# Two sparse-attention and MLP layers on one core: four rounds of the first MLP cut into three ranges of inner blocks, and the weight conversion spread to match

## The chip, the cores and the metric

One core of one Trainium2 chip runs the whole program. The metric is the device time of one execution in microseconds (us); lower is better. Where the text says PE, DVE, ACT, POOL and SP, it means the tensor, vector, scalar, GpSimd and sync engines, as the profile does.

## The reference

```python
# attention: q, k, v are [4, 8, 576, 64]
scores = scale * q @ k.T
thresh = max(scores, axis=-1) - tau
scores = where(scores >= thresh, scores, -1e9) - max(scores)
attn = exp(scores) / (sum(exp(scores)) + 1e-9)
x = (attn @ v)  ->  [2304, 512]
# first MLP, 512 -> 2048 -> 512
h = x @ w_in
g = where(h >= 1, h, where(h <= -1, 0, (h + 1)**2 / 4))
x = g @ w_out
# second MLP, other weights
h = x @ w_in2
g = h * clip(h + 3, 0, 6) / 6
out = g @ w_out2
```

## The kernel before

**Attention.** There are 16 jobs, one for a batch and a pair of heads, and each has five blocks of query rows. One block of one job is here called a step: 80 steps, 0 to 79, with job j at steps 5j to 5j+4. In a step PE makes the scores (L335), DVE copies them out with a minimum of the negated scores (L348), ACT takes the exponential (L360), DVE masks and sums (L369), PE transposes the result through the identity (L284), ACT copies that out (L397 and others) and PE multiplies with v (L433). A job has nine tiles of scores, so nine L348 and nine L369; the profile records a second short read of the accumulator for each.

**First MLP beside attention.** While attention still runs, the program works on six groups of 256 rows (groups 0 and 1 are batch 0, 2 and 3 batch 1, 4 and 5 batch 2). A round is one group with a list of inner blocks, each 128 of the 2048 hidden columns; only blocks 0 to 9 are treated in this part. For each inner block, `em_h` makes the hidden tile on PE in 12 matmuls of 256 columns (L676; three products for each of four slices, since values are split into a high and a low part), and ACT, DVE and POOL make its activation (L685 to L694). Two `em_part` calls then multiply it with the output weights, 6 matmuls each (L738), one for each half of the output columns. These add up over the round in one PSUM bank, "Q3". At the end of a half the sum is copied out and stored to `x2p` (L747 to L752). If the round's first block isn't block 0, the earlier partial sum is loaded first into the one buffer `before` (L732) and added at the copy (L747). At the start of a round `split_x` makes the high and low part of the group's rows: four pairs of ACT L656 and DVE L657, into buffers that the round before has to have left. The sequence of blocks over all rounds is numbered n = 0 to 59.

**How the two are woven.** The attention code is a generator; at each of its yields (22 in five steps) the MLP generator `dense1` gets a credit of 0.57, and each slice of its work costs 0.33, so that a block n with two output parts costs 2.64. Before a round of a group, `dense1` asks `ready(g)`: all four jobs of the group's batch must have been normalized. Batch 1 is jobs 4 to 7, and the last of them is normalized at step 44. Until then `dense1` yields nothing, and the credit is cut at 3. What is left when attention ends runs after it without attention beside it. A scheduler then moves instructions within each engine's order.

**Weights.** Each inner block needs a piece of the input weights and one of the output weights, 20 pieces in this part. They arrive as 64-bit floats and are converted on the chip: ACT L118, L121, L139, POOL L122, L137, L141, DVE L129 and L135. `pace(n)` says how many pieces are to be done at block n: `FIRST` before the first block, then `RATE` for each block.

**After attention.** The rest of the groups and the second MLP follow with matmuls of 512 columns (L676, L718) from about 500 us to the end.

Of the kernel before, what the change touches and what calls it, by code (L numbers as in the profile page):

```python
# [18 lines left out]
def kernel(  # L19
# [24 lines left out]
    NG = (NB - 1) * MAIN // GRP  # L44
# [3 lines left out]
    NF1 = 10  # L48
# [22 lines left out]
    def narrow(t, g):  # L71
        return t[g // 2][:, :, (g % 2) * GRP:(g % 2 + 1) * GRP]
# [594 lines left out]
    def em_h(key, m, f):  # L667
        cnt["h"] += 1
        n = GRP if key[2] == 1 else WIDE[key[1]]
        h = bank(H_TAGS[cnt["h"] % len(H_TAGS)])[:, 0:n]  # L670
        wh, wl = wsp["i", m, f]
        x = 0
        for kk in range(KD):
            xh, xl = xs[key][kk]
            for l, r in ((wh, xh), (wh, xl), (wl, xh)):
                mm = T.matmul(h, l[:, kk * 128:(kk + 1) * 128], r, start=(x == 0), stop=(x == 3 * KD - 1))  # L676
                if x % 3 == 0:
                    pin_mlp(mm)
                x += 1
            if kk < KD - 1:  # L680
                yield 0.33
        hp_, hb = (mt, HOLD) if key[2] == 1 else (wide["g"], MLAG + 1)
        r = hp_.tile([128, n], F32, tag="r", name="r", bufs=2)
        if m == 0:
            S.activation(out=r, in_=h, func=ACTF.Relu, scale=0.5, bias=half)  # L685
            S.activation(out=r, in_=r, func=ACTF.Square)  # L686
            vlast = V.scalar_tensor_tensor(out=r, in0=r, scalar=1.0, in1=h, op0=ALU.min, op1=ALU.max)  # L687
        else:
            S.activation(out=r, in_=h, func=ACTF.Relu, bias=three)  # L689
            vlast = V.scalar_tensor_tensor(out=r, in0=r, scalar=6.0, in1=h, op0=ALU.min, op1=ALU.mult)  # L690
        gh = hp_.tile([128, n], F32R, tag="gh", name="gh", bufs=hb)
        gl = hp_.tile([128, n], F32R, tag="gl", name="gl", bufs=hb)
        x = S.activation(out=gh, in_=r, func=ACTF.Copy)  # L693
        y = G.tensor_tensor(out=gl, in0=r, in1=f32(gh), op=ALU.subtract)  # L694
        gs[key, f] = (gh, gl)
        if not mode["att"]:
            pins.update(S=x, V=vlast, G=y)
# [24 lines left out]
    def em_part(key, half, f):  # L722

        gh, gl = gs[key, f] if half == 0 else gs.pop((key, f))
        wh, wl = wsp["o", 0, f]
        g, fs = ROUNDS[key[3]]
        dst = narrow(x2p, g)[:, 2 * half:2 * half + 2, :]
# [61 lines left out]
                nc.sync.dma_start(out=out[b * SEQ + MAIN:(b + 1) * SEQ, :], in_=ob[64 * e:64 * e + 64, :])  # L789

    HALF = NF1 // 2
    ROUNDS = [(g, list(range(f, f + HALF))) for f in (0, HALF) for g in range(2)]
    ROUNDS += [(g, list(range(NF1))) for g in range(2, NG)]
    before = {}
    hs = [(r, f) for r, (g, fs) in enumerate(ROUNDS) for f in fs]
    n_h = len(hs)
    outs = [(r, half, f) for r, (g, fs) in enumerate(ROUNDS) for half in range(2) for f in fs]
    OFF = NF1 + 2 * MLAG - 3
    steps, o = [], 0
    while o < len(outs):  # L800
        n = len(steps)
# [8 lines left out]
    def round_key(r):  # L810
        return (0, ROUNDS[r][0], 1, r)

    def dense1(ready, ahead):

        for n, l in enumerate(steps[:n_h]):
            r, f = hs[n]
            key = round_key(r)
            if key not in xs:
                while not ready(key[1]):
                    yield None  # L820
                split_x(key)
            ahead(n, f)
            yield from em_h(key, 0, f)
            if f == ROUNDS[r][1][-1]:
                xs.pop(key)
                if r + 1 < len(ROUNDS) and ready(ROUNDS[r + 1][0]):
                    split_x(round_key(r + 1))
            if n == n_h - 3 and not mode["att"]:
                split_x((0, NB - 1, 2))
            yield 0.33  # L830
            for i, (r, half, f) in enumerate(l):
                if i == 1:
                    pace(n + 0.5)
                yield from em_part(round_key(r), half, f)
                yield 0.33
# [86 lines left out]
    by_use = sorted(first_use, key=lambda x: (first_use[x], x))  # L922
    weights.items += [(kind, 0, f) for kind, f in by_use]

    def pace(n):
        goal = min(2 * len(by_use), 2 * FIRST + 2 * RATE * n)
        while mode["att"] and 2 * weights.done + weights.mid < goal:
            weights.half()

    def ahead1(n, f):  # L930
        weights.upto(sum(1 for x in by_use if first_use[x] < n + 2))
        pace(n)
        if not mode["att"] and weights.done < 2 * KF:
            weights.half()

    part1 = dense1(ready, ahead1)
    share = 0.57
    FIRST, RATE = 5, 0.85
    credit = 0.0
    for _ in attention():  # L940
        if not mode["mlp"]:
# [110 lines left out]
```

## Time and profile before

| what | value |
|---|---|
| median of 3 runs | 1119.37 us (1119.02 to 1120.56) |
| the profiled execution's own time | 1118.67 us |
| its span, first to last instruction | 1116.9 us |
| PE busy | 1087.4 us (97%) |
| DVE, ACT, POOL busy | 583.3, 614.0, 438.4 us |
| granted TensorE clock, mean | 0.992 |

Matmuls are pipelined, so that a busy PE isn't the same as a PE that starts a matmul as often as it can; how far apart the matmuls start is read from the chain of work in order of time. The stretches used below begin at the first DVE row L348 of steps 24, 39, 44 and 78: at 102.5, 207.3, 237.8 and 445.4 us.

### The profile page before, as it was taken

The page shows a single profiled execution, that of the slowest core. Times are in us where ns is not written, and L with a number is a line of the kernel's source. Part 1 is how long each engine was busy: PE and PEld are TensorE (multiplying, and loading weights), DVE is VectorE, ACT ScalarE, POOL GpSimd, SP SyncE. Part 2 cuts the span into 40 slices and gives each one's busy share as a digit, 9 for nine tenths or more (in the row PEclk, how much of TensorE's full clock was granted, in tenths as well). Part 3 has the DMA queues.
Part 4 walks back from the last instruction along what each step waited for, and adds up shares of the span by engine and source line. Part 5 has one row for each costly group of instructions (what it writes and reads, how often), then busy time and mean ns, then how long its engine had stood idle before and what let it go on. Part 6 is the DMA issues. An engine that isn't in the chain of part 4 may idle for free.

```text
span 1116.9 us, 17595 instructions
## 1 busy us (share of the span) xinstructions
PE 1087.4 (97%) x6478; PEld 882.1 (79%) x6478; DVE 583.3 (52%) x1204; ACT 614.0 (55%) x1215; POOL 438.4 (39%) x382
## 2 busy tenths in 40 slices
PE   7998889999999999999999999999999999999998
PEld 5555667777878877888889888888888888898886
DVE  5899887876666656355536765558411111211111
ACT  5777886866667666556557766555432222333222
POOL 0233767622222111155627566567522222222221
PEclk9999889999999999999999999999999999999999
DMA  6454445433222110025222544533010110010001
GB/s 165 118 100 107 124 120 150 103 93 74 63 59 62 43 43 22 12 67 170 77 94 78 157 143 145 158 114 111 24 38 1 33 38 1 10 38 8 13 1 38
DMA packets 140230, 84.26 MB, mean 75 GB/s; under 512 B 99440, under 2 KB 123248, under 8 KB 140144
## 3 DMA queue, kind: packets, MB, share of 16 engines
q1 hardware_dynamic: 138800, 82.84, 27.0%
q8 instruction: 51, 0.84, 0.3%
q10 hardware_dynamic: 1344, 0.30, 0.1%
q14 instruction: 35, 0.29, 0.1%
HBM read 65.73 MB, written 17.37 MB: 74 GB/s over the span
## 4 chain that ended last, share of the span: by engine, by line
PE 88%; DVE 7%; ACT 2%; POOL 1%; issue 1%; SPq 1%; DMA 0%; DVEq 0%; POOLq 0%; ACTq 0%
PE Q L676 35%; PE P L718 28%; PE Q L738 7%; PE Q L433 6%; PE P L335 6%; PE Q L284 5%; DVE p L348 2%; DVE p L369 2%; ACT e L360 1%; DVE xl L657 1%; SPq L227 0%; PE Q L904 0%; DVE th L363 0%; DVE w_c L135 0%; DMA w_raw<-in_moe_w_out_dram 0%
## 5 line engine op out<-in xcount | busy, mean ns | idle before, releaser
L694 POOL TENSOR_TENSOR gl<-r,gh 128x512 fp32r<-128x512 f32 (+1 forms) x190 | 202.6, 1067 | 501.0 <-ACT gh L693 500.5
L676 PE MATMUL Q<-xh,wih 128*128 128x512 f32 (+1 forms) x760 | 262.0, 345 | 0.9 <-DVE r L687 0.7
L676 PE MATMUL Q<-xl,wih 128*128 128x512 f32 (+1 forms) x760 | 257.1, 338 | 0.0
L676 PE MATMUL Q<-xh,wil 128*128 128x512 f32 (+1 forms) x760 | 256.8, 338 | 0.0
L690 DVE SCALAR_TENSOR_TENSOR r<-r,Q 128x512 f32<-128x512 f32 (+1 forms) x80 | 50.7, 633 | 249.4 <-ACT r L689 249.3
L693 ACT ACTIVATE gh<-r 128x512 fp32r<-128x512 f32 (+1 forms) x190 | 99.9, 526 | 125.3 <-PE P L718 53.2
L676 PEld LDWEIGHTS Q<-xh,wih 128*128 128x128 f32 x760 | 144.1, 190 | 24.3 <-issue 4.2
L676 PEld LDWEIGHTS Q<-xl,wih 128*128 128x128 f32 x760 | 144.2, 190 | 16.0
L676 PEld LDWEIGHTS Q<-xh,wil 128*128 128x128 f32 x760 | 144.0, 190 | 15.5
L348 DVE TENSOR_SCALAR_CACHE_REDUCE p<-P 128x576 f32<-128x576 f32 x144 | 104.0, 751 | 53.3 <-PE Q L284 41.0
L369 DVE SCALAR_TENSOR_TENSOR p<-p,th,e 128x576 f32<-128x576 f32 x144 | 122.8, 873 | 15.1 <-ACT e L360 9.5
L689 ACT ACTIVATE r<-Q,three 128x512 f32<-128x512 f32 (+1 forms) x80 | 51.4, 643 | 142.9 <-PE Q L676 138.3
L360 ACT ACTIVATE e<-p,nm 128x576 f32<-128x576 f32 x144 | 108.9, 775 | 34.5 <-DVE p L348 33.6
L687 DVE SCALAR_TENSOR_TENSOR r<-r,Q 128x256 f32<-128x256 f32 (+1 forms) x110 | 54.8, 498 | 125.7 <-ACT r L686 122.4
L284 PE MATMUL Q<-ident,p 128*128 128x128 f32 x656 | 107.9, 282 | 9.8 <-ACT Gf L397 6.5
L718 PE MATMUL P<-woh,gh 128*128 128x512 f32 x288 | 111.9, 390 | 0.6 <-DVE ob L776 0.6
L718 PE MATMUL P<-wol,gh 128*128 128x512 f32 x288 | 112.2, 390 | 0.0
L718 PE MATMUL P<-woh,gl 128*128 128x512 f32 x288 | 111.0, 390 | 0.0
L335 PE MATMUL P<-kt,qt 64*128 64x288 f32 (+1 forms) x640 | 99.5, 429 | 11.0 <-DVE p L348 9.0
L284 PEld LDWEIGHTS Q<-ident,p 128*128 128x128 f32 x656 | 73.6, 141 | 46.3 <-ACT Gf L397 14.0
L137 POOL TENSOR_TENSOR w_c<-w_c,w_raw 128x512 int32<-128x512 int32 x64 | 89.5, 1400 | 41.3 <-DVE w_c L135 23.0
L397 ACT ACTIVATE Gf<-Q 128x512 f32<-128x512 f32 x128 | 74.4, 596 | 33.5 <-PE Q L284 32.8
(91 smaller groups left out, 1840.1 us busy)
## 6 DMA issues: line engine op xcount, KB each, us to landing
w_raw<-in_moe_w_in_dram SPq DMA_DIRECT2D x32, 512.0 KB
w_raw<-in_moe_w_out_dram SPq DMA_DIRECT2D x32, 512.0 KB
vn<-in_v_dram SPq DMA_DIRECT2D x32, 128.0 KB
x2p<-ob SPq DMA_DIRECT2D x16, 256.0 KB
x2d<-ob SPq DMA_DIRECT2D x16, 256.0 KB
xst<-x2d SPq DMA_DIRECT2D x16, 256.0 KB
out_dram<-ob SPq DMA_DIRECT2D x16, 256.0 KB
xst<-xd SPq DMA_DIRECT2D x15, 256.0 KB
```

What stands on the lines that cost most here:

```text
L137: x = G.tensor_tensor(out=c.bitcast(I32), in0=c.bitcast(I32), in1=r, op=ALU.add)
L284: x = T.transpose(out, in_, ident)
L335: mm = T.matmul(o, qt[j][r, c], kt[j][r, k0:k0 + HS], start=True, stop=True, skip_group_check=True)
L348: reads(V.tensor_scalar(out=p[:, x], in0=s[:, :, 0:HS], scalar1=-1.0, scalar2=3e38, op0=ALU.mult, op1=ALU.min, accum_out=nm[:, x:x + 1]), ...
L360: pins["S"] = S.activation(out=e, in_=p[:, x], func=ACTF.Exp, bias=nm[:, x:x + 1], scale=-1.0)
L369: pins["M"] = V.scalar_tensor_tensor(out=p[:, x], in0=p[:, x], scalar=th[:, x:x + 1], in1=e, op0=ALU.is_le, op1=ALU.mult, accum_out=zt[j][ ...
L397: S.activation(out=f[:, h, :, d0:d0 + 128], in_=tm.rearrange("p (c n) -> p c n", c=4), func=ACTF.Copy)
L676: mm = T.matmul(h, l[:, kk * 128:(kk + 1) * 128], r, start=(x == 0), stop=(x == 3 * KD - 1))
L693: x = S.activation(out=gh, in_=r, func=ACTF.Copy)
L694: y = G.tensor_tensor(out=gl, in0=r, in1=f32(gh), op=ALU.subtract)
L718: T.matmul(a, l, r, start=(first and x == 0), stop=(last and x == 2))
L738: mm = T.matmul(o, l, r, start=(f == fs[0] and x == 0 and i == 0), stop=(f == fs[-1] and x == 2 and i == 1), skip_group_check=True)
```

## The change

Rounds 0 to 3 were (group 0, blocks 0 to 4), (1, 0 to 4), (0, 5 to 9), (1, 5 to 9), and groups 2 to 5 had all ten blocks in one round each. Now the rounds are (0, 0 to 3), (1, 0 to 3), (0, 4 to 6), (1, 4 to 6), (2, 0 to 6), (3, 0 to 6), then 7 to 9 for groups 0, 1, 2 and 3, then groups 4 and 5 as before: 12 rounds in place of 8, with the same 60 blocks n. The conversion's pace is 0.75 for a block up to n = 12 and 0.45 behind it, in place of 0.85.

```diff
     HALF = NF1 // 2
-    ROUNDS = [(g, list(range(f, f + HALF))) for f in (0, HALF) for g in range(2)]
-    ROUNDS += [(g, list(range(NF1))) for g in range(2, NG)]
+    PLAN = (((0,1),0,4),((0,1),4,7),((2,3),0,7),((0,1,2,3),7,10))
+    ROUNDS = [(g, list(range(a, z))) for gs_, a, z in PLAN for g in gs_]
+    ROUNDS += [(g, list(range(NF1))) for g in range(4, NG)]
...
     def pace(n):
-        goal = min(2 * len(by_use), 2 * FIRST + 2 * RATE * n)
+        goal = min(2 * len(by_use), 2 * FIRST + 2 * RATE * min(n, KNEE) + 2 * LATER * max(n - KNEE, 0))
...
-    FIRST, RATE = 5, 0.85
+    FIRST, RATE, KNEE, LATER = 5, 0.75, 12, 0.45
```

The first block of group 2 was n = 20 and is now n = 14. On PE, before, step 41 begins with the scores (L335), v (L433), a transpose (L284), and then has the 12 matmuls of a hidden tile (L676):

```order
L335 MATMUL P_2946<-kt,qt 128x288
L335 MATMUL P_2947<-kt,qt 128x288
L335 MATMUL P_2946<-kt,qt 128x288
L335 MATMUL P_2947<-kt,qt 128x288
L433 MATMUL Q_2896<-Gf,vn_97 64x320 x8
L433 MATMUL Q_2896<-Gt,vn_97 64x320 x2
L284 MATMUL Q_2914<-ident,p 128x128 x3
L676 MATMUL Q_2790<-xh,wih_1758 128x256
L676 MATMUL Q_2790<-xl,wih_1758 128x256
L676 MATMUL Q_2790<-xh,wil_1759 128x256
```

Of the change, PE's order at step 41 and the beginning of step 42:

```order
L335 MATMUL P_2748<-kt,qt 128x288
L335 MATMUL P_2749<-kt,qt 128x288
L335 MATMUL P_2748<-kt,qt 128x288
L335 MATMUL P_2749<-kt,qt 128x288
L433 MATMUL Q_2724<-Gf,vn_97 64x320 x8
L433 MATMUL Q_2724<-Gt,vn_97 64x320 x2
L284 MATMUL Q_2736<-ident,p 128x128 x4
L335 MATMUL P_2781<-kt,qt 128x288
L335 MATMUL P_2782<-kt,qt 128x288
L335 MATMUL P_2781<-kt,qt 128x288
L335 MATMUL P_2782<-kt,qt 128x288
```

The MLP's matmuls have left this place: steps 40 to 43 hold attention alone, and the next hidden tile (n = 14, group 2) stands in step 44.

DVE's order at step 69 before: scores out (L348), an activation (L687), threshold, mask, and the sums of a finished job (L452 to L456).

```order
L348 TENSOR_SCALAR p,nm<-P_5079 128x576
L687 SCALAR_TENSOR_TENSOR r<-r,Q_4964 128x256
L363 TENSOR_SCALAR th<-nm,taus 128x1
L369 SCALAR_TENSOR_TENSOR p,z<-p,th,e 128x576
L452 TENSOR_SCALAR z<-z 128x9
L453 RECIPROCAL rp<-z 128x9
L456 STREAM_TRANSPOSE rq<-rp 128x32
```

Of the change, DVE's order at step 69 up to the mask:

```order
L348 TENSOR_SCALAR p,nm<-P_4964 128x576
L293 STREAM_TRANSPOSE qt<-qn 128x576
L309 STREAM_TRANSPOSE kt<-kn 128x640
L657 TENSOR_TENSOR xl<-xu,xh 128x256
L687 SCALAR_TENSOR_TENSOR r<-r,Q_4748 128x256
L363 TENSOR_SCALAR th<-nm,taus 128x1
L747 TENSOR_TENSOR ob<-Q_4831,before 128x512
L369 SCALAR_TENSOR_TENSOR p,z<-p,th,e 128x576
```

What has come is a split of a further round (L657) and the addition of an earlier partial sum (L747), ahead of the mask in the same in-order queue; the two transposes come from a neighbouring step.

Counted in the two orders by attention steps (the MLP's matmuls of 256 columns on PE, L676 and L738; on DVE the converted pieces, L135, the splits, L657 of 256 columns, the additions, L747, the plain copies, L751, and the activations, L687 of 256 columns):

| steps | matmuls before, now | pieces | splits | additions | copies | activations |
|---|---|---|---|---|---|---|
| 24 to 38 | 300, 258 | 14, 13 | 12, 16 | 0, 0 | 2, 2 | 14, 12 |
| 39 to 43 | 114, 12 | 2, 0 | 4, 0 | 1, 0 | 0, 0 | 5, 2 |
| 44 to 77 | 789, 777 | 0, 3 | 16, 28 | 3, 12 | 3, 2 | 32, 31 |
| 78 to the end | 621, 777 | 44, 44 | 8, 12 | 0, 0 | 1, 2 | 24, 31 |

## Rows read from the trace of the kernel before

**Rows 1.** The page: slices of the span, busy tenths and the granted clock.

```profile
PE   7998889999999999999999999999999999999998
DVE  5899887876666656355536765558411111211111
PEclk9999889999999999999999999999999999999999
```

**Rows 2.** Busy time by stretch (x instructions), PE clock, DMA share, GB/s.

```profile
core 0: us, PE busy (x) PEld busy (x) DVE busy (x) ACT busy (x) POOL busy (x), PEclk, DMA share, GB/s
20.00:100.00 80.00, 74.27 (x536) 45.45 (x535) 71.43 (x192) 62.93 (x129) 22.94 (x19) 1.00 0.53 125
102.50:207.30 104.80, 91.90 (x640) 70.14 (x640) 89.98 (x199) 81.71 (x181) 72.61 (x62) 0.92 0.50 130
207.30:237.80 30.50, 29.46 (x230) 23.20 (x229) 25.87 (x62) 23.25 (x53) 15.63 (x15) 1.00 0.32 78
237.80:445.40 207.60, 207.60 (x1615) 165.25 (x1614) 131.96 (x366) 134.97 (x301) 44.98 (x46) 1.00 0.24 56
496.60:1100.00 603.40, 603.40 (x2958) 511.51 (x2958) 229.72 (x309) 267.31 (x469) 262.41 (x210) 1.00 0.22 68
```

**Rows 3.** Who PE waited for, 102.5 to 237.8 us: total us, times, longest.

```profile
PE Q L284 <- ACT Gf L397: 4.0, 5, 1.6
PE P L335 <- DVE p L348: 3.4, 2, 2.1
PE Q L284 <- DVE p L369: 1.8, 1, 1.8
PE Q L738 <- DVE ob L751: 1.4, 1, 1.4
```

**Rows 4.** Three stretches at half clock, columns as in rows 2.

```profile
112.90:119.80 6.90, 5.22 (x21) 2.38 (x21) 6.90 (x13) 5.45 (x11) 4.46 (x5) 0.51 0.23 79
143.60:150.50 6.90, 5.62 (x23) 4.18 (x24) 6.90 (x20) 4.76 (x12) 3.57 (x3) 0.51 0.46 129
177.80:181.20 3.40, 3.40 (x18) 3.40 (x18) 3.25 (x9) 2.89 (x5) 2.16 (x3) 0.50 0.93 268
```

**Rows 5.** The chain of work: start us, us, what; 60 and 24 matmuls of 256 columns.

```profile
496.58 7.19 PE Q L738 x60
...
176.93 4.64 PE Q L738 x24
```

**Rows 6.** The chain from 102.5 to 207.3 us, shares by line.

```profile
by line: PE Q L738 12.3%; PE Q L676 10.6%; PE Q L433 10.4%; DVE p L348 6.8%; PE P L335 6.7%; issue 5.5%; DVE xl L657 4.8%; PE Q L284 4.3%; DVE p L369 3.7%; DMA w_raw<-in_moe_w_out_dram 3.7%; POOL wol L141 3.4%; POOL w_c L137 3.0%; DVE w_c L
```

**Rows 7.** DVE groups by form, 107 to 238 us: busy us, mean ns, idle before.

```profile
L369 DVE SCALAR_TENSOR_TENSOR p<-p,th,e 128x576 f32<-128x576 f32 x35 | 34.4, 1004 | 2.6 <-ACT e L360 1.8
L135 DVE SCALAR_TENSOR_TENSOR w_c<-w_raw,w_c 128x512 uint32<-128x512 uint32 x16 | 12.3, 767 | 0.1
L129 DVE TENSOR_SCALAR w_c<-w_c 128x512 uint32<-128x512 uint32 x15 | 9.3, 622 | 0.5 <-POOL w_c L122 0.5
L657 DVE TENSOR_TENSOR xl<-xu,xh 128x256 fp32r<-128x256 f32 x15 | 7.6, 526 | 1.7 <-ACT xh L656 1.7
```

**Rows 8.** DVE groups by form, 238 to 445 us.

```profile
L369 DVE SCALAR_TENSOR_TENSOR p<-p,th,e 128x576 f32<-128x576 f32 x61 | 48.6, 816 | 7.4 <-ACT e L360 4.8
L348 DVE TENSOR_SCALAR_CACHE_REDUCE p<-P 128x576 f32<-128x576 f32 x61 | 43.8, 752 | 36.9 <-PE Q L284 31.8 <-PE P L335 5.0
L687 DVE SCALAR_TENSOR_TENSOR r<-r,Q 128x256 f32<-128x256 f32 x33 | 13.7, 416 | 21.4 <-ACT r L686 18.4 <-POOL xu L488 2.7
L363 DVE TENSOR_SCALAR th<-nm,taus 128x2 f32<-128x2 f32 x27 | 6.1, 227 | 0.8
L657 DVE TENSOR_TENSOR xl<-xu,xh 128x256 fp32r<-128x256 f32 x14 | 5.3, 418 | 0.0
L369 DVE DVE_READ_ACCUMULATOR p<-p,th,e 128x1 f32 x61 | 5.0, 82 | 0.0
L309 DVE STREAM_TRANSPOSE kt<-kn 128x640 f32<-128x640 f32 x5 | 4.0, 802 | 0.0
L293 DVE STREAM_TRANSPOSE qt<-qn 128x576 f32<-128x576 f32 x5 | 3.9, 775 | 1.3 <-PE P L335 1.3
```

**Rows 9.** Instructions of line L348 (copies and reads, 18 in a job) by stretch.

```profile
20.00:100.00 80.00, 27.65 (x75) 1.00 0.53 125
```

**Rows 10.** All DVE groups by form, the addition of the earlier sum.

```profile
L747 DVE TENSOR_TENSOR ob<-Q,before 128x512 f32<-128x512 f32 x4 | 2.7, 684 | 0.0
```

## Prediction, made before the run

> **What bounds the kernel now.** I read the slices of the page first [rows 1]. PE is at 9 tenths or more from the fifth part of the span on; before that DVE is the fuller engine. The busy times by stretch say it more sharply [rows 2]. From 237.8 to 445.4 us PE is busy 207.60 of 207.60 us, and from 496.6 to 1100 us all 603.40, at full clock. There the time is PE's own work, and the change adds and removes no matmul, it only puts some elsewhere. So a gain can come only from what PE loses between 102.5 and 237.8 us, where attention, the MLP and the conversion run together. There PE was busy 91.90 of 104.80 us and 29.46 of 30.50 us, DVE 89.98 and 25.87. The table of waits shows what PE lost: 4.0 us to ACT's copies behind its transposes, 3.4 to the scores' copies, 1.8 to a mask, 1.4 to the copy of a finished half [rows 3]. And three times the granted clock fell to the lower level, 1.2 GHz: 6.90, 6.90 and 3.40 us at about 0.5 [rows 4].
>
> The price of an MLP matmul of 256 columns at full clock comes from the chain: 60 of them in 7.19 us, 0.120 us each. The run of 24 that lies mostly in the third of the slow stretches took 4.64 us, 0.193 each [rows 5].
>
> **The change, part by part.** I sum in attention steps, because attention's own work is the same. The table behind the diff counts the rest.
>
> *The wait that is added.* Group 2 now comes at n = 14, not n = 20, but its batch is still done only at step 44. A block costs 2.64 of credit and a step brings 22/5 times 0.57, or 2.51. The first five blocks cost half, the sixth three quarters. Counted from step 24, where batch 0 is done, n = 14 is reached about step 36 (29.7 of credit), and `dense1` then yields nothing until 44; n = 20 before took until about step 42 (45.5). The order, which spreads this a little, says the same: 12 MLP matmuls in steps 39 to 43 where there were 114. Nothing of the MLP is lost, only moved: 156 matmuls more stand behind step 78, where no attention is left to fill beside them and PE is the bound. They cost 156 times 0.120, **+18.7 us**. Against this, attention comes to its end earlier, by the three terms that follow.
>
> *Steps 39 to 43, five steps, one job.* They took 30.50 us [rows 2]. With the MLP gone DVE sets the pace, as in the attention from 20 to 100 us, where it was busy 71.43 of 80 us [rows 2]. One job's DVE rows [rows 8] are nine copies and nine masks with their reads, 9 x (0.752 + 0.082 + 0.816 + 0.082) = 15.6 us (the copies' reads taken as the masks'), five thresholds 1.1, two transposes 1.6, two activations 0.8: 19.1 us, and about 0.7 for a job's sums, 19.8. The early attention checks it: 75 of the 18 rows that a job has, 4.17 jobs, in 80 us, 19.2 us a job [rows 9]. So **-10.7 us**; 12.0 if the two transposes slip into the next step, 8.5 if the chain PE, ACT, DVE leaves gaps.
>
> *Steps 24 to 38.* The change is meant to relieve DVE here, but it hardly does: 13 pieces in place of 14. One piece is 0.767 + 0.622 = 1.39 us of DVE, and two activations fewer are 0.8, while four splits more are 4 x 0.526 = 2.1 us [rows 7]. DVE comes out even. What falls is PE: 42 matmuls, 5.0 us. If PE ended each wait all of it would come out, if the other engines did none would. PE's lines hold 44% of the chain of this stretch (12.3 + 10.6 + 10.4 + 6.7 + 4.3) [rows 6], so I take 0.44 x 5.0, **-2.2 us**, between 0 and -5.0.
>
> *Steps 44 to 77.* PE was never idle, and 12 matmuls fewer give **-1.4 us**. DVE gets three pieces (at 1.39), twelve splits (at 0.418), nine additions (at 0.684) and one copy less: +14.7 us on 131.96 of 207.60 [rows 2, 8, 10], to 71%. That is less than the 85% at which PE lost little in the stretch just before [rows 2]. The twelve additions wait for the load of `before`, and masks stand behind them in DVE's queue. The bank Q3 has to be emptied at each half, and the order puts other PE work behind these ends. I take **+1.0**, between 0 and 4: the nine new ends of a half would cost PE 1.4 us each if none were covered [rows 3], and all but one of the sixteen now are.
>
> *The start of group 2 at step 44.* n = 14 waits for job 7's normalization and a split with no MLP work queued ahead on PE: **+0.5**, between 0 and 3.
>
> *Behind step 78* one more round's split and seven activations lie beside matmuls; DVE was busy 229.72 of 603.40 us there [rows 2], so nothing, and at most the four splits, 1.7 us.
>
> Sum: 18.7 - 10.7 - 2.2 - 1.4 + 1.0 + 0.5 = +5.9 us on the profiled execution's 1118.67, 1124.6. The median of the runs is 0.7 above that execution, so I predict **1125.3 us**.
>
> **The rivals.**
>
> *A. The crowded stretch loosens, faster.* The masks there took 1004 ns on average and 816 ns behind it [rows 7, 8], so a conversion costs DVE more than its own time. For 35 masks that is 6.6 us, over 16 pieces 0.41 a piece. The Trainium skill, "SBUF — State Buffer", section "SBUF: two separate sides", says that a GpSimd instruction and a DVE instruction with two SBUF inputs exclude each other through a shared port pair, for the whole instruction. The longer masks agree with it. Were the two later half-clock stretches also to go, with half their 6.90 + 3.40 us, then with the full 5.0 of PE work and 1.8 for the piece that goes, steps 24 to 38 would give -12.0 in place of -2.2, and the time would be 1115.5 us. It decides for faster once these steps take more than 10 us less (8.1 us bring the sum to zero, 2.2 more are needed to be told from no change). Against it: 13 of 14 pieces stay.
>
> *B. Nothing to measure.* The removed matmuls of steps 24 to 38 come out whole (-5.0) and the five steps run at 18.5 us (-12.0): +1.8, 1121.2 us. For it speaks that PE was already at 97% in steps 39 to 43, so little is wasted either way.
>
> *C. Slower still.* In the steps without MLP the clock falls and the additions hold up DVE's masks. One half-clock stretch as those seen costs up to half of 6.90, 3.4 us; with 4 for steps 44 to 77 and 3 at step 44 the sum is +14.8, 1134.2 us. The Trainium skill, "TensorE: Matmul & The Clock Gate", Part 1 on the clock gate, says that the reduced clock is the default and steady activity lifts it, which would let the thinned steps fall. Against it: attention alone kept 1.00 from 20 to 100 us with PE busy 74.27 of 80 [rows 2].
>
> *D. The change doesn't do what it says.* By the order it doesn't: the conversions for blocks 7 to 9 are said to come only with them, yet the pace has all 20 pieces done by n = 26, and blocks 7 begin at n = 28. Three pieces move, to steps 44 to 77. That is in my sum.
>
> **How the numbers follow.** What a measurement can tell here is about 0.2%, 2.2 us. My case, between 1121.6 and 1129, has 0.43; A 0.24; B 0.18; C 0.15. So faster 0.24, same 0.18, slower 0.58. The range reaches into A and C: 1115 to 1132, leaving out about 2 in 10. The likeliest case alone reaches from 1121.6 to 1129.
>
> **What would show it.** In the changed profile, a hole in L676 and L738 of about 20 us that ends when group 2's split (L656, L657) begins, with PE below full and DVE near 9 tenths; attention's last L348 earlier by 10 to 15 us than now; and a longer run of 256-column matmuls behind it. If the half-clock stretches after 140 us are gone, A has come; if new ones stand in the hole, C. The prediction is wrong if steps 24 to 38 take under 99 us in place of 104.8, or if PE idles for longer than now between 238 and 440 us.

## The result, and the profile after

The changed kernel takes **1126.68 us** (median of 4 runs, 1124.91 to 1127.9), the kernel before 1119.70 beside it: ratio 1.0059, interval [1.0043, 1.0075], slower by 0.6%. The profiled execution took 1126.03 us, its span 1124.2. Below, the first L348 of steps 24, 39, 44 and 78 again bounds the stretches: 102.6, 205.4, 225.4 and 433.7 us.

The page of the change, slices of the span [rows 1]:

```profile
PE   7988899899999999999999999999999999999998
...
DVE  5889899877777664462535855657410211211111
...
PEclk9999889999999999999999999999999999999999
```

DVE is fuller in the sixth and seventh slice (140 to 197 us) and from the tenth to the thirteenth. The stretches say more; columns as in rows 2:

```profile
20.00:100.00 80.00, 74.02 (x537) 45.40 (x533) 71.07 (x194) 63.02 (x130) 22.99 (x19) 1.00 0.53 124
102.60:205.40 102.80, 86.80 (x601) 63.97 (x603) 96.11 (x202) 77.85 (x173) 68.29 (x57) 0.93 0.50 130
205.40:225.40 20.00, 18.75 (x138) 12.50 (x133) 15.51 (x46) 15.42 (x33) 4.97 (x5) 1.00 0.35 77
225.40:433.70 208.30, 206.84 (x1600) 164.09 (x1600) 146.61 (x392) 140.66 (x319) 56.53 (x53) 1.00 0.34 89
```

Steps 24 to 38 took 102.8 us (104.8 before), 39 to 43 took 20.0 (30.5), 44 to 77 took 208.3 (207.6), and from step 78 to the end it was 690.5 (671.5). Attention is through 11.6 us earlier, and 19.0 us come back behind it. In the first of these stretches DVE rose from 89.98 us of 104.80 to 96.11 of 102.80, while PE fell to 86.80. From 238 to 440 us, where PE of the kernel before was busy all 202.00 us, it now stands idle for 1.26:

```profile
238.00:440.00 202.00, 200.74 (x1553) 159.35 (x1553) 140.19 (x375) 136.57 (x310) 55.14 (x52) 1.00 0.33 86
```

The MLP's matmuls in the change, L676 by stretch, and then L738; the (x) behind PE's time counts them:

```profile
102.60:205.40 102.80, 21.73 (x144) 19.22 (x144) 0.93 0.50 130
205.40:225.40 20.00, 3.34 (x24) 2.98 (x24) 1.00 0.35 77
225.40:433.70 208.30, 54.91 (x384) 48.27 (x384) 1.00 0.34 89
433.70:1124.00 690.30, 358.64 (x1728) 291.17 (x1728) 1.00 0.20 64
```

```profile
102.60:205.40 102.80, 15.59 (x102) 13.24 (x102) 0.93 0.50 130
205.40:225.40 20.00, 0.00 (x0) 0.00 (x0) 1.00 0.35 77
225.40:433.70 208.30, 59.90 (x385) 50.17 (x386) 1.00 0.34 89
433.70:1124.00 690.30, 32.72 (x234) 29.92 (x234) 1.00 0.20 64
```

The same view of before has 180, 48, 399 and 1656 of L676, and 115, 60, 386 and 162 of L738. So the change has 49, 84 and 16 matmuls fewer in the three stretches, and 144 more behind step 78. Their price is unchanged, 7.19 us for 60 in the chain [rows 5]:

```profile
498.87 7.19 PE Q L738 x60
```

Who PE waited for in the change, 102.6 to 225.4 us [rows 3], total, times, longest:

```profile
PE Q L284 <- ACT Gf L397: 4.7, 6, 1.6
PE P L335 <- DVE p L348: 3.2, 2, 2.1
PE Q L676 <- DVE r L687: 3.2, 4, 2.0
```

And from 433 to 520 us, behind attention, where PE of the kernel before had no such wait:

```profile
PE Q L676 <- DVE r L687: 1.5, 2, 0.8
```

The half-clock stretches of the change [rows 4]; the third of before, at 177.8, has no successor:

```profile
113.40:120.20 6.80, 5.46 (x21) 2.38 (x21) 6.80 (x13) 5.11 (x11) 4.37 (x5) 0.50 0.25 68
140.70:147.50 6.80, 5.79 (x24) 4.76 (x25) 6.70 (x16) 4.55 (x9) 4.66 (x4) 0.50 0.41 99
```

DVE's groups in the change, 102.6 to 225.4 us [rows 7]:

```profile
L369 DVE SCALAR_TENSOR_TENSOR p<-p,th,e 128x576 f32<-128x576 f32 x36 | 37.0, 1043 | 2.8 <-ACT e L360 1.5
...
L657 DVE TENSOR_TENSOR xl<-xu,xh 128x256 fp32r<-128x256 f32 x15 | 10.7, 749 | 0.0
L135 DVE SCALAR_TENSOR_TENSOR w_c<-w_raw,w_c 128x512 uint32<-128x512 uint32 x13 | 9.4, 726 | 0.0
L363 DVE TENSOR_SCALAR th<-nm,taus 128x2 f32<-128x2 f32 x16 | 9.4, 585 | 0.3
```

A split (L657) took 749 ns on average here, where it took 526 in a like stretch before [rows 7] and 418 behind it [rows 8]. The thresholds (L363) grew too; before, from 107 to 238 us, they took 463 ns:

```profile
L363 DVE TENSOR_SCALAR th<-nm,taus 128x2 f32<-128x2 f32 x16 | 7.4, 463 | 0.3
```

### The profile page after: what moved, and what is told of

Its sections match the earlier page's. It is cut to its first block, busy times and chain, and to the rows that moved or that the text cites. A ratio compares the mean times of both kernels' runs of the same rounds, so it can differ in the third digit from the quotient of the medians.

```text
span 1124.2 us, 17699 instructions
## 1 busy us (share of the span) xinstructions
PE 1088.1 (97%) x6478; PEld 881.9 (78%) x6478; DVE 595.3 (53%) x1228; ACT 618.6 (55%) x1231; POOL 441.3 (39%) x382
## 4 chain that ended last, share of the span: by engine, by line
PE 85%; DVE 8%; ACT 4%; issue 1%; DMA 1%; POOL 1%; SPq 1%; DVEq 0%; ACTq 0%; POOLq 0%
PE Q L676 34%; PE P L718 28%; PE Q L738 7%; PE Q L433 6%; PE P L335 5%; PE Q L284 4%; DVE p L348 2%; DVE p L369 2%; ACT e L360 1%; DVE xl L657 1%; ACT Gf L397 1%; DVE th L363 1%; SPq L227 0%; PE Q L905 0%; DVE w_c L135 0%
## 5 line engine op out<-in xcount | busy, mean ns | idle before, releaser
L694 POOL TENSOR_TENSOR gl<-r,gh 128x512 fp32r<-128x512 f32 (+1 forms) x190 | 206.7, 1088 | 470.3 <-ACT gh L693 465.1
L676 PE MATMUL Q<-xh,wih 128*128 128x512 f32 (+1 forms) x760 | 261.3, 344 | 4.7 <-DVE r L687 4.7
L676 PE MATMUL Q<-xl,wih 128*128 128x512 f32 (+1 forms) x760 | 257.2, 338 | 0.0
L676 PE MATMUL Q<-xh,wil 128*128 128x512 f32 (+1 forms) x760 | 257.0, 338 | 0.0
L676 PEld LDWEIGHTS Q<-xh,wih 128*128 128x128 f32 x760 | 144.2, 190 | 30.3 <-DVE r L687 6.2
L676 PEld LDWEIGHTS Q<-xl,wih 128*128 128x128 f32 x760 | 144.4, 190 | 15.8
L676 PEld LDWEIGHTS Q<-xh,wil 128*128 128x128 f32 x760 | 144.3, 190 | 15.3
L369 DVE SCALAR_TENSOR_TENSOR p<-p,th,e 128x576 f32<-128x576 f32 x144 | 126.4, 898 | 13.9 <-ACT e L360 7.9
L348 DVE TENSOR_SCALAR_CACHE_REDUCE p<-P 128x576 f32<-128x576 f32 x144 | 104.3, 752 | 45.6 <-PE Q L284 36.3
L284 PE MATMUL Q<-ident,p 128*128 128x128 f32 x656 | 105.6, 282 | 13.0 <-ACT Gf L397 8.1
L687 DVE SCALAR_TENSOR_TENSOR r<-r,Q 128x256 f32<-128x256 f32 (+1 forms) x110 | 54.8, 498 | 118.3 <-ACT r L686 113.9
L284 PEld LDWEIGHTS Q<-ident,p 128*128 128x128 f32 x656 | 73.6, 141 | 48.4 <-ACT Gf L397 15.5
L335 PE MATMUL P<-kt,qt 64*128 64x288 f32 (+1 forms) x640 | 99.4, 429 | 11.0 <-DVE p L348 9.0
L685 ACT ACTIVATE r<-Q,half 128x256 f32<-128x256 f32 (+1 forms) x110 | 58.7, 535 | 51.2 <-PE Q L676 45.8
```

Of the source, the lines that this page charges most:

```text
L284: x = T.transpose(out, in_, ident)
L335: mm = T.matmul(o, qt[j][r, c], kt[j][r, k0:k0 + HS], start=True, stop=True, skip_group_check=True)
L348: reads(V.tensor_scalar(out=p[:, x], in0=s[:, :, 0:HS], scalar1=-1.0, scalar2=3e38, op0=ALU.mult, op1=ALU.min, accum_out=nm[:, x:x + 1]), ...
L369: pins["M"] = V.scalar_tensor_tensor(out=p[:, x], in0=p[:, x], scalar=th[:, x:x + 1], in1=e, op0=ALU.is_le, op1=ALU.mult, accum_out=zt[j][ ...
```

## The experiments

**How they are read.** The number of matmuls is fixed, so a stretch that holds n matmuls fewer ought to be shorter by n times 0.120 us. What it isn't shorter by, PE has lost. The table gives for each run its change of duration against the profiled execution of before in us, in brackets the change in matmuls of L676 and L738, and behind the stroke what PE lost more than before (the first less 0.120 times the second). For the change, steps 24 to 38: -2.1 + 49 x 0.120 = 3.8. The matmuls of a stretch are priced at full clock, so a loss is good to about 1 us. The change's four losses sum to 7.8 us, while its span is 7.3 us longer, since the counts at the bounds don't quite cancel.

The bounds blur one thing more. Attention's products with v (L433) are not counted, and they can fall on either side of a bound. The first row is of the change, where step 39 begins at 205.40 us, and the second of before, where it begins at 207.31:

```profile
204.32 1.95 PE L433 MATMUL Q<-Gf,vn 128*64 128x256 f32 x16 [0.16 <-ACT Gf L397]
208.01 1.95 PE L433 MATMUL Q<-Gf,vn 128*64 128x256 f32 x16
```

Ten products, at 0.11 us each, lie ahead of the bound in the change that lay behind it before. With them the change's 3.8 and -0.4 become 2.7 and 0.7. In the same way e7's 3.6 and 0.3 become 2.5 and 1.4, e5's 7.6 and -1.0 become 5.8 and 0.8 (sixteen products), and e3's 3.2 and 4.7 become 1.8 and 6.1 (thirteen, at step 44). The sums of two such stretches don't move. In the other runs it is 0.7 us or less.

| run | median us, ratio to before | 24 to 38 | 39 to 43 | 44 to 77 | 78 to end |
|---|---|---|---|---|---|
| the change | 1126.7, 1.0059 | -2.1 (-49) / 3.8 | -10.5 (-84) / -0.4 | +0.8 (-16) / 2.7 | +19.0 (+144) / 1.7 |
| e1_plan_only | 1136.4, 1.0159 | +1.4 (-40) / 6.2 | -8.2 (-90) / 2.6 | +4.3 (-15) / 6.1 | +19.4 (+144) / 2.1 |
| e2_pace_only | 1122.5, 1.0033 | -0.6 (-6) / 0.1 | +1.4 (-10) / 2.6 | +2.1 (+16) / 0.2 | -0.1 (0) / -0.1 |
| e3_no_hole | 1127.6, 1.0079 | -2.9 (-27) / 0.3 | +3.1 (-1) / 3.2 | +8.0 (+28) / 4.7 | +0.4 (0) / 0.4 |
| e5_seven | 1134.9, 1.0143 | -6.0 (-113) / 7.6 | -3.4 (-20) / -1.0 | +4.8 (-16) / 6.8 | +20.2 (+144) / 2.9 |
| e7_share_050 | 1124.0, 1.0046 | -0.9 (-37) / 3.6 | 0.0 (-3) / 0.3 | -2.2 (-17) / -0.1 | +8.6 (+54) / 2.1 |
| e8_share_066 | 1120.5, 1.0014 | +5.3 (+29) / 1.8 | -2.9 (-18) / -0.7 | -1.2 (-9) / -0.2 | -0.5 (-3) / -0.2 |
| e9_no_resplit | 1122.0, 1.0029 | -7.0 (-39) / -2.4 | -8.5 (-92) / 2.6 | -1.5 (-15) / 0.3 | +19.8 (+144) / 2.5 |
| e10_early_pace | 1131.2, 1.0113 | +1.0 (-41) / 5.9 | -8.2 (-90) / 2.6 | +0.1 (-16) / 2.0 | +19.4 (+144) / 2.1 |
| e11_no_addition | 1127.5, 1.0075 | -2.3 (-49) / 3.6 | -9.4 (-84) / 0.7 | +0.7 (-16) / 2.6 | +19.5 (+144) / 2.2 |
| e12_keep_split | 1123.8, 1.0048 | -3.0 (-19) / -0.7 | +4.3 (+24) / 1.4 | 0.0 (-7) / 0.8 | +1.9 (0) / 1.9 |
| e13_after_055 | 1125.0, 1.0064 | -4.6 (-50) / 1.4 | -8.2 (-80) / 1.4 | +0.8 (-15) / 2.6 | +19.0 (+144) / 1.7 |
| e14_after_059 | 1130.9, 1.0106 | +3.3 (-25) / 6.3 | -10.9 (-108) / 2.1 | +0.3 (-16) / 2.2 | +19.1 (+144) / 1.8 |

The intervals of the ratios are 0.0008 to 0.0016 to either side. Before took 1118.5 to 1118.7 us beside these runs. The stretches are those of one execution; that of e12 was the fastest of its five, 3.1 us below their median.

**The two parts alone, and two other plans.** My theory was that of the prediction: work held back by the hole and done behind step 78. The rivals were the pace and the mere number of rounds.

```diff
e1: the change, with the pace of before
-    FIRST, RATE, KNEE, LATER = 5, 0.75, 12, 0.45
+    FIRST, RATE = 5, 0.85
e2: the rounds of before, with the pace of the change
-    FIRST, RATE = 5, 0.85
+    FIRST, RATE, KNEE, LATER = 5, 0.75, 12, 0.45
e3: groups 0 and 1 finish before 2 and 3 begin
+    PLAN = (((0,1),0,4),((0,1),4,7),((0,1),7,10),((2,3),0,10))
e5: two ranges
+    PLAN = (((0,1,2,3),0,7),((0,1,2,3),7,10))
```

> The new rounds with the old pace (0.85 a block throughout). By the order, 258 and 12 MLP matmuls of 256 columns in steps 24 to 38 and 39 to 43, 759 behind step 78 (621 in the kernel before), and 13 pieces converted in steps 24 to 38, as in the changed kernel. My theory (the rounds empty steps 39 to 43, and what is missing there is paid at 0.120 us a matmul behind attention): 138 x 0.12 = 16.6 us later at the end, about 12 to 13 us won before it, so 1123 to 1127 us. Rival (the slower pace is what costs): back near 1120 us.

> The old rounds with the new pace (0.75, then 0.45 from n = 12). The MLP matmuls stand where they stood before (300, 114, 789, 621), since each block's weights are still forced when the block comes; 12 pieces in steps 24 to 38 and 4 in 39 to 43, before 14 and 2. My theory: the same as before within 2 us, 1118 to 1122 us. Rival (pace): 1124 us or more. A third view (fewer conversions in the crowded steps are worth 1.4 to 1.8 us a piece): 1116 to 1117 us.

> The changed kernel, but groups 0 and 1 also take blocks 7 to 9 before group 2 begins (ranges 0 to 3, 4 to 6, 7 to 9), and groups 2 and 3 take all ten in one round. Group 2 comes at n = 20 again. There are 10 rounds in place of 12 (8 before), 8 additions of earlier sums (4 before, 12 changed). MLP matmuls in the four stretches: 270, 102, 831, 621. My theory: the hole is gone and so is the debt behind step 78; what is left is the cost of two rounds more in the crowded steps (8 splits at 0.53 to 1.1 us of DVE, 4 additions at 0.7), at most 10 us of DVE, of which under half shows: 1120 to 1124 us. Rival (the added rounds with their loads and additions are the cost, not the hole): 1125 us or more.

> The changed kernel, but the four groups take blocks 0 to 6 in one round each, then 7 to 9: the hole stays (group 2 at n = 14), the small rounds at the start go. 10 rounds. In steps 24 to 38 there are 8 splits (12 before, 16 changed), 12 pieces, 198 matmuls; in 39 to 43 72 matmuls; 759 behind step 78. My theory: the debt of 138 x 0.12 = 16.6 us stays, while steps 24 to 38 lose about 8 us of DVE work against before and take about 97 us (104.8 before, 102.8 changed) and steps 39 to 43 about 25: 1122 to 1127 us, no better than the changed kernel by more than 3 us. Rival (rounds are the cost): 1119 to 1121 us.

e1 missed on both sides: 1136.4 us. The new pace isn't what made the change slower; with the new rounds it saves 10 us, with the old ones it costs 4 (e2, 1122.5, just above my range). e3 missed too, its rival's time came, and it is what turned the theory: without the hole, and with nothing more behind step 78 (+0.4 us), it is as slow as the change, 1127.6. So a kernel can be as slow as this without a hole; that the hole costs the change nothing doesn't follow. Nor are e3's splits the whole of it: the largest loss is in steps 44 to 77, with 16 splits as before, and 2.0 us of it are PE's waits for pieces of weights converted late (L139, L141). e5 came out 8 us above its range. It takes 113 matmuls out of steps 24 to 38, 13.6 us of work, and gets 6.0 us for them, or 7.8 with the products that moved in.

From here on the theory was PE's losses: what is moved is paid at one place and given back at the other, and the kernel is slower by what PE loses beside that.

**More or less MLP beside attention, in the kernel before.** The credit of a yield up to step 44 (share is 0.57):

```diff
-        credit = min(credit + share, 3.0)
+        credit = min(credit + (0.50 if mode["t"] < 45 else share), 3.0)
```

> The rounds and pace of before, with a credit of 0.50 for a yield in place of 0.57 up to step 44: by the order 30 MLP matmuls fewer in steps 24 to 38 and 18 fewer in 39 to 43, and 51 more behind step 78. Theory (PE's losses decide, since the number of matmuls is fixed: a matmul put behind step 78 costs 0.120 us there, and one taken from steps 39 to 43 gives 0.120 back, while one taken from steps 24 to 38 gives back less, because DVE is the fuller engine there): +6.1 behind step 78, -2.2 in steps 39 to 43, between -1.6 and 0 in steps 24 to 38, so 1120 to 1123 us. Rival (the crowd loosens when the MLP is thinned): steps 24 to 38 give back 6 us or more, 1117 us or less.

> The rounds and pace of before, with a credit of 0.66 up to step 44: by the order 24 MLP matmuls more in steps 24 to 38, 24 fewer in 39 to 43 where a short hole opens before group 2, and the same number behind step 78. Theory (PE's losses decide, a hole in itself costs nothing): steps 39 to 43 give 2.9 us back, steps 24 to 38 pay 1 to 2.9 us, so 1115.5 to 1119 us. Rival (a hole costs, or the crowd gets worse by more than the matmuls' own time): 1120 us or more.

e7 is 1 us above its range, and far from the rival: thinned by 37 matmuls, steps 24 to 38 gave back 0.9 us of 4.4, or 2.0 with the products that moved in. e8 ended 1.5 us above the theory's range, and the rival's time came out; 1.5 us of it lay ahead of step 24, where PE had the same 635 instructions as before. Its short hole cost nothing in its own steps: 18 matmuls fewer in steps 39 to 43 made them 2.9 us shorter.

**The repeated splits, and the two halves of the pace, in the change.**

```diff
e9: later rounds leave out the split
+    seen, latest = set(), {}
...
-        r = xs.setdefault(key, [])
+        r = xs.setdefault(key, [latest[x] for x in range(KD)] if ph == 1 and g in seen else [])
...
-            r.append((hi, lo))
+            r.append((hi, lo)); seen.add(g if ph == 1 else -1); latest[kk] = (hi, lo)
e10: the early pace of before, the later one of the change
-    FIRST, RATE, KNEE, LATER = 5, 0.75, 12, 0.45
+    FIRST, RATE, KNEE, LATER = 5, 0.85, 12, 0.45
```

> The changed kernel, in which the later rounds of groups 0 to 3 leave out the split of their rows and read the parts that lie in the buffers: by the order 8 splits fewer in steps 24 to 38 and 16 fewer in steps 44 to 77. The hole and the work behind step 78 stay. Theory (what the change lost beside the moved matmuls is the splits in the crowded stretch and in the steps behind 44): most of the 6 us that PE lost there comes back, 1119 to 1123 us. Rival (the additions, or too little PE work as cover, lost it): 1125 to 1127 us.

> The changed kernel with the early pace of before (0.85 up to n = 12) and its own later pace (0.45). The changed rounds with the whole pace of before took 1136.4 us, 10 more than the change. If the early pace costs them (pieces of weights that meet the splits in steps 24 to 38): 1133 to 1137 us. If the late one (three pieces right behind step 44): 1126 to 1129 us.

e9 leaves out the second splits, ACT's part (L656) and DVE's (L657), and most of the later rounds then multiply another group's rows. It held: 1122.0 us, 4.7 less than the change. PE's loss went from 3.8 to -2.4 us in steps 24 to 38 and from 2.7 to 0.3 in 44 to 77. The stretches of e9:

```profile
103.40:201.20 97.80, 83.23 (x601) 62.16 (x602) 92.41 (x192) 75.83 (x166) 68.24 (x58) 0.97 0.54 134
201.20:223.20 22.00, 19.18 (x139) 12.06 (x139) 15.58 (x46) 14.90 (x33) 5.18 (x5) 1.00 0.34 70
223.20:429.30 206.10, 206.10 (x1600) 164.05 (x1600) 141.73 (x379) 137.88 (x305) 53.90 (x54) 1.00 0.31 80
```

DVE lost 3.70 us of work in the first (96.11 to 92.41), and the stretch became 5.0 us shorter. Not all of that is the change's own: before has second splits of groups 0 and 1 too. By the order the change has 4 splits more than before in steps 24 to 38, but 4 fewer in 39 to 43, and 12 more in 44 to 77; e9 leaves out 8, none and 16. Part of what e9 gains ahead of step 39 is also lost again right behind it: over steps 24 to 43 together PE's loss falls from 3.4 to 0.2 us, 3.2 for eight splits. In proportion (an estimate), the four that the change moved into steps 24 to 38 cost at most 1.6 us of its losses, and the twelve new ones in 44 to 77 cost 1.8. What e9 still is over before, 3.5 us, stands in steps 39 to 43 and behind 78; no run explains the part in 39 to 43.

e10 fell between its two cases, 1131.2: the early pace costs the change 4.6 us and the late one 5.2 more (e1). The late part has one place, steps 44 and 45. First e1, then e10:

```profile
230.80:244.40 13.60, 12.23 (x96) 9.67 (x96) 12.95 (x32) 10.31 (x23) 5.34 (x6) 1.00 0.52 118
```

```profile
230.40:240.20 9.80, 9.80 (x79) 7.55 (x80) 9.05 (x28) 6.57 (x16) 1.01 (x1) 1.00 0.44 76
```

In e1 the pieces stand right there: POOL has 5.34 us of work in place of 1.01, PE 1.37 us of idle time, and the two steps are 3.8 us longer, over 17 more PE instructions.

**Additions left out, splits kept.**

```diff
e11: the change
-            if fs[0]:
+            if False:
                 before[key] = mt.tile([128, 512], F32, tag="before", name="before", bufs=1)
e12: before
+    kept, old = {}, {2: 0, 3: 1, 4: 2, 5: 3}
...
-        r = xs.setdefault(key, [])
+        r = xs.setdefault(key, kept.get(g, []) if ph == 1 else [])
...
-                pool, n, bufs = mt, GRP, 1
+                pool, n, bufs, kept[g] = mt, GRP, 2, r; kept.pop(old.get(g), None)
...
-    ROUNDS += [(g, list(range(NF1))) for g in range(2, NG)]
+    ROUNDS += [(g, list(range(f, f + HALF))) for g in range(2, NG) for f in (0, HALF)]
...
-    OFF = NF1 + 2 * MLAG - 3
+    OFF = NF1 + 2 * MLAG - 5
```

> The changed kernel without the additions of the earlier partial sums: no load of the earlier sum, and the twelve ends of a half in steps 44 to 77 are plain copies, six on DVE and six on ACT; the output lacks the earlier blocks of these rounds. Theory (the repeated splits made the loss of PE in steps 44 to 77, 2.4 of 2.7 us by the run that left them out): steps 44 to 77 give back 0 to 1 us, 1125 to 1127 us. Rival (the additions and the load they wait for hold up the masks, as I had it in the prediction, +1.0 and up to 4): 1122.5 to 1124.5 us.

> Before's plan for groups 0 and 1, but with two sets of split buffers, so that the second rounds of groups 0 and 1 read the parts that the first rounds made: 8 splits fewer, 4 of them in steps 24 to 38 and 4 in 39 to 43. To make room the groups 2 to 5 have their ten blocks in two rounds of five with the same split (8 additions more), and an output part comes one block earlier. Theory (a split in the stretch with the conversion costs 0.6 to 0.8 us of PE's time, behind it 0.15; an addition next to nothing): steps 24 to 43 give back 2.4 to 4.5 us, 1114 to 1117 us. Rival (the splits of before are covered, or the additions cost what the splits give): 1118 to 1121 us.

e11 excludes the additions: PE's loss in steps 44 to 77 stays at 2.6 us without them, and its 1127.5 lies 0.5 above the range. e12 missed, 1123.8. It was meant as a kernel that beats both. Its four splits fewer gave PE 0.7 us in steps 24 to 38, far less than e9's 0.8 us for each split (6.2 us for eight), and PE lost 1.4, 0.8 and 1.9 us later. So a split has no fixed price. Three edits stand together in it, so which of them cost that is open.

**Neighbours of the change.** The same kernel with a credit of 0.55 and of 0.59 up to step 44, which by the order moves 12 matmuls between steps 24 to 38 and 39 to 43 and nothing else. By the trace, whose steps are cut at DVE's rows, e14 has 24 more in the first and 24 fewer in the second, and e13 1 fewer and 4 more.

> The changed kernel with a credit of 0.55 in place of 0.57 up to step 44. By the order 12 MLP matmuls go from steps 24 to 38 into 39 to 43 and nothing else is counted differently; the same pieces, splits and work behind step 78. Theory (a matmul in steps 39 to 43 costs its 0.12 us and one taken from 24 to 38 gives about half of that back, all else stays): 1126 to 1128.5 us. Rival (where single splits meet conversions in steps 24 to 38 decides, more than the amounts): more than 2.5 us away from 1126.7, to either side.

> The changed kernel with a credit of 0.59 up to step 44. By the order the last 12 MLP matmuls of steps 39 to 43 stand in steps 24 to 38 instead, which leaves none in 39 to 43; the rest is counted as in the change. Theory (as for the run with 0.55, with the other sign): steps 39 to 43 give 1.4 us back, 24 to 38 pay 0.7 to 1.4, 1125 to 1127 us. Rival (single meetings of splits and conversions decide): more than 2.5 us away from 1126.7.

The rival held for e14: 1130.9 us, 4.2 above the change. e13, 1125.0, lies below the theory's range but within 2.5 us of the change, so it decides for neither. Up to step 34 e14 runs like the change, each step starting within 0.2 us of it. Step 35 then starts at 189.7 us in place of 172.7. At this place POOL and DVE of the change:

```profile
169.57 1.28 POOL L137 TENSOR_TENSOR w_c<-w_c,w_raw 128x512 int32<-128x512 int32 x1 [0.63 <-DVE z L452]
170.82 0.79 POOL L122 TENSOR_SCALAR w_c<-w_c 128x512 f32<-128x512 f32 x1
173.79 1.30 POOL L141 TENSOR_TENSOR wil<-w_c,wih 128x512 fp32r<-128x512 f32 x1 [2.18 <-ACT wih L139]
```

```profile
170.00 2.22 DVE L657 TENSOR_TENSOR xl<-xu,xh 128x256 fp32r<-128x256 f32 x3
172.14 0.68 DVE L751 COPY ob<-Q 128x512 f32<-128x512 f32 x1
```

And of e14 POOL, DVE, and the one waiting PE row between 164 and 185 us, with its idle time in brackets:

```profile
169.53 1.28 POOL L137 TENSOR_TENSOR w_c<-w_c,w_raw 128x512 int32<-128x512 int32 x1 [0.63 <-DVE z L452]
170.78 0.79 POOL L122 TENSOR_SCALAR w_c<-w_c 128x512 f32<-128x512 f32 x1
171.56 1.41 POOL L141 TENSOR_TENSOR wil<-w_c,wih 128x512 fp32r<-128x512 f32 x1
```

```profile
169.95 3.29 DVE L657 TENSOR_TENSOR xl<-xu,xh 128x256 fp32r<-128x256 f32 x3
173.17 0.68 DVE L751 COPY ob<-Q 128x512 f32<-128x512 f32 x1
```

```profile
173.90 0.58 PE L738 MATMUL Q<-gh,woh 128*128 128x256 f32 x1 [4.07 <-DVE ob L751]
```

In e14 a conversion's L141 stands right behind L122 on POOL, and the three splits beside it take 3.29 us in place of 2.22. It is the third of them that differs. The first row is of the change, where POOL is idle beside it, the second of e14, where L141 runs:

```profile
171.81 0.41 DVE L657 TENSOR_TENSOR xl<-xu,xh 128x256 fp32r<-128x256 f32 x1
171.76 1.48 DVE L657 TENSOR_TENSOR xl<-xu,xh 128x256 fp32r<-128x256 f32 x1
```

The copy that empties Q3 (L751) is behind the splits in DVE's queue, and the next output part on PE behind the copy. It starts at 173.90 us, where the change's starts at 172.87, so the longer split is worth 1.0 us here. PE of e14 idles 4.07 us, but the change's PE waits at this place too, 1.92 us, and does six transposes meanwhile:

```profile
171.61 0.66 PE L284 MATMUL Q<-ident,p 128*128 128x128 f32 x4 [1.74 <-ACT xu L439]
172.44 0.44 PE L284 MATMUL Q<-ident,p 128*128 128x128 f32 x2 [0.18 <-ACT Gt L411]
172.87 0.39 PE L738 MATMUL Q<-gh,woh 128*128 128x256 f32 x1
```

The order of the instructions differs as well, which the counts by steps don't show: in the change the copy of step 35's scores (L348) comes next on DVE, in e14 four activations (L687) and the next four splits stand ahead of it, and some of them wait for ACT. First a row of the change, then one of e14:

```profile
172.74 0.74 DVE L348 TENSOR_SCALAR_CACHE_REDUCE p<-P 128x576 f32<-128x576 f32 x1
181.20 0.42 DVE L687 SCALAR_TENSOR_TENSOR r<-r,Q 128x256 f32<-128x256 f32 x1 [5.62 <-ACT r L686]
```

In e14 the granted clock then is half, from 173.5 us on:

```profile
173.50:176.90 3.40, 3.00 (x14) 3.00 (x15) 2.04 (x5) 0.42 (x1) 1.87 (x2) 0.50 0.70 142
```

e1 has the same wait at this place, 3.7 us. From step 48 on e14 is 4.7 us later than the change. How these 4.7 us divide between the longer split, the order and the clock, no run shows.

## Why the prediction came out as it did

I predicted 1125.3 us and the time is 1126.68. The case I took as likeliest came, with the hole, attention's earlier end and the debt behind it. But the terms that held are those that cancel each other; the reasons for the remainder were partly wrong.

*Behind step 78*: +18.7 predicted, 19.0 measured. The count was off: the order says 156 matmuls more, the trace 144, which is 17.3 us. The other 1.7 are mostly PE's waits for activations between 433.7 and 500 us (L687, 1.5 us), where I had put nothing. Two small errors balance. The waits are no accident of this kernel: all nine with 54 or 144 matmuls more behind step 78 wait 1.5 to 1.9 us there for DVE or ACT, and before, e2, e3 and e8 don't (e12: 0.7 us).

*Steps 39 to 43*: -10.7 predicted, -10.5 measured. e14, with no MLP matmul there, took 19.6 us, close to the 19.8 that I had for DVE's pace. The sign that I named was wrong, though: DVE isn't near 9 tenths but at 15.51 of 20.00 us, PE at 18.75, so that DVE sets the pace there isn't shown. And 84 matmuls at 0.120 are 10.1 us, so this term is only the other side of the debt. In these steps themselves the hole costs nothing that stands out: with the shifted products counted, PE's loss there is 0.7 to 2.6 us in the kernels with the hole, 1.4 to 2.6 in those without it (e2, e3, e7, e12) and -0.3 beside e8's short one.

*Steps 24 to 38*: -2.2 predicted, -2.1 measured, and the agreement is luck. The step that failed is "DVE comes out even". A split took 749 ns there, not the 526 I priced, and with the splits, masks and thresholds DVE's load rose by 6.1 us. Without eight splits the stretch was 5.0 us shorter (e9), though DVE's busy time fell by only 3.7. I took 44% of 5.0 us for PE's share; 49 matmuls went, 5.9 us, of which 2.1 came out, or 3.2 with the products with v that moved in. The upper bound of 0 was too low: with the same pieces and splits this stretch came out at -4.6 (e13) and at +3.3 us (e14).

*Steps 44 to 77*: +0.1 with the restart, measured +0.8. The price was put on the wrong item. The additions that I feared cost nothing (e11), and with sixteen splits left out, twelve of them new, 2.4 of the 2.7 us that PE lost were gone (e9). One of the two signs of being wrong that I named did come: PE idles longer than before between 238 and 440 us, by 1.26 us.

*The rivals.* A did not come, although one of its signs did: the half-clock stretch near 180 us went, and steps 24 to 38 gave only 2.1 us. e3 and e12 had no such stretch behind 120 us and PE still lost there what it lost before, within 0.7 us. That a DVE instruction grows beside POOL's can be read from the rows all the same: the same split took 0.41 us in the change and 1.48 in e14. The rule of the Trainium skill, "SBUF — State Buffer", section "SBUF: two separate sides", on the port pair shared by DVE and GpSimd agrees with it; no run takes the port away, so the cause is read from the rows, not isolated. C came neither as a clock fall in the hole (1.00 there) nor through the additions. D was as the order said: 13 pieces in the crowded stretch.

So the change isn't slower because PE stands empty in the hole. What is shown: PE loses 7.8 us more than before, 3.4 of it in steps 24 to 43, 2.7 in 44 to 77 and 1.7 behind step 78. The last part comes with the work paid back there. Of the 2.7 us most goes with the splits (e9); the additions have no part in it, and the old pace makes these rounds slower, not faster (e1, e10). What is argued: that the loss in steps 24 to 43 is partly the splits moved into the crowded steps, at most 1.6 us by the estimate above, and partly MLP work taken out of a stretch that DVE sets, as e5 and e7 suggest for two other kernels. How it divides stays open, since a small difference of order as in e14 moves the stretch by as much.

## What to carry to other kernels

Where the amount of TensorE work is fixed, price each stretch by its matmuls and look only at what TensorE loses beside them: a hole that is paid back later costs little beyond the matmuls themselves (here 1.5 to 1.9 us of waits where they are paid back), and work taken out of a stretch that another engine sets gives back only part of its price. Count each repeated preparation (here a split for each further round) at its price in the crowded stretch, not at its price alone. And run a neighbour or two before believing a term of a few us in a woven schedule: a credit of 0.59 in place of 0.57, which moved 24 matmuls and the order around them, changed this one by 4.2 us.

## What the runs showed of the hardware

The same DVE subtraction of 128x256 took 0.42 us on average in steps 44 to 77 of before [rows 8] and 0.75 in steps 24 to 43 of the change; one took 0.41 us with POOL idle beside it and 1.48 us in e14 beside a POOL instruction (L141) of 1.41 us. The copy behind it, and PE's output part behind the copy, came 1.0 us later.

That fewer stretches at half clock gained so little was new to me too. e3 and e12 each had one of 6.8 us in steps 24 to 38, where before had three, 17.2 us together, and these steps were no more than 3.0 us shorter, with 27 and 19 matmuls fewer. The change and e14 say it more sharply. From 140.7 to 147.5 us the change ran at a granted clock of 0.50 and e14 at 1.00, with DVE busy for 6.70 of the 6.80 us in both, and steps 31 to 34 started within 0.1 us of each other. The row of e14:

```profile
140.70:147.50 6.80, 3.75 (x29) 3.07 (x29) 6.70 (x16) 4.59 (x9) 4.65 (x4) 1.00 0.46 125
```
